# Handing over batch 0's 1 / standard deviation two steps of batch 1's front end earlier, and giving the feed forward's evictions the highest priority

## The chip, the cores and the metric

One Trainium2 chip, one core. The metric is the device time of one execution of the kernel in microseconds. The kernel before takes 1086.92 us, the median of 3 runs from 1086.22 to 1087.01.

## The reference

Eight batches of an attention whose keys and values are averaged over 8 positions, then a block that mixes with a Fourier transform and ends with a feed forward. Cut to what matters, with B = 8, S = 576 positions and 512 channels:

```python
x = attention(q, pooled k, pooled v)          # 8 x 576 x 512
X = np.fft.fft(np.fft.fft(x, axis=1), axis=2)
u = x + np.real(X)
mu = np.mean(u, axis=-1, keepdims=True)
var = np.mean((u - mu) ** 2, axis=-1, keepdims=True)
un = (u - mu) / np.sqrt(var + 1e-06)
ch = np.maximum(un @ w_ch1, 0.0) @ w_ch2      # 512 -> 2048 -> 512
out = u + ch
```

Because the Relu lets a positive factor through, the kernel feeds the centred `u - mu` to the feed forward and multiplies what comes out by `rb`, the 1 / standard deviation. So `rb` is not needed by the first matmul of a block of the feed forward, only after its last one.

## The kernel before, in words

**Two kinds of work.** Each batch b has a front end, the generator `fe(b)`, which yields after each step. Its steps are the scores (psS, L351), their maximum, subtraction and exponential (L356, L365, L367, L368 to L371), transposes (psT, psV, psR), the values (psX, L439, read out by lines 443 to 452), the transform along the channels (psA L558, psB L584, their parts read out at L538) and along the sequence (psQ, psP, L601), the mean (psM, L656 and L657), the centred U (L661) and its two parts `unh` (ScalarE, L645) and `unl` (the rest, L646, two tiles on VectorE and two on GpSimd). Then comes "z", and behind it a tail that makes `rb`. For batch 0 the tail squares (L695 to L698), sums over the partitions with ten small matmuls into psVar (L721), takes the inverse root by three Newton rounds on 128x5 elements (VectorE, L726, L728, L730 to L733), spreads it over a diagonal in X (L736, L737), multiplies that by a matrix of ones (TensorE, L739) and copies it to `rb` (ScalarE, L740).

The feed forward, `ffn`, goes over blocks of columns. One step f of a block takes 128 of the 2048 inner channels. It makes g by twelve matmuls (w1h by unh, w1h by unl, w1low by unh, L775), `hh` = Relu(g) on ScalarE (L779), `hl` = max(g, 0) - hh on VectorE (L780), and then twelve matmuls into four banks acc0 to acc3 (w2h by hh, w2low by hh, w2h by hl, L759). `hh` and `hl` have two buffers each, g has two banks, acc has four banks and no spare: the next block's first matmul into a bank waits for VectorE to have multiplied it by `rb` (L804) and added it to U (L805). Batch 0 has four blocks of eight steps, 288 columns each: (columns 0 to 287, f 0 to 7), (288 to 575, f 0 to 7), then the same two with f 8 to 15. Batches 1 to 6 run in blocks of 384 columns and 16 steps, batch 7 again in blocks of 288. In all 208 steps. In the names, `g_0_7` is step 7 of the block at column 0, `acc_288` or `g_288` the block at column 288.

**Weights.** While batch 0 runs, the weights are prepared chunk by chunk: `prep_w` scales, masks and casts (ScalarE L196, L198, L206; VectorE L201, L202), subtracts on GpSimd (L207) and stores the low part by a DMA of SP's queue (L208). `load_low` reads the low parts back by SP's queue (L217), two steps ahead, for every step.

**What sets the order.** All instructions of an engine run in one order fixed at build time. A scheduler takes, of those instructions whose inputs are there by its own estimate, the one that was traced first, so the tracing order is the priority; a few edges (`issue_after`) pin some of them. The driver traces batch 0's front end as far as "z", then eleven `prep_w`, then batch 1's front end step by step. Among batch 1's steps it hands in the tail of batch 0's: one step (the squares) ahead of step TAIL0, the rest ahead of step TAIL1. From step 20 on, steps of batch 2's front end are handed in too. Only behind all this the feed forward is traced, and so it fills what the front end leaves free. From there on the function `advance` traces later front ends in step with the blocks.

The lines of the driver that count:

```python
fe2, n2 = fe(2), 0
for n, _ in enumerate(fe1):
    if n in (TAIL0, TAIL1):
        next(fe0)
    if n == TAIL1:
        for _ in fe0:
            pass
```

Of the kernel before, what the change touches and what calls it, by code (L numbers as in the profile page):

```python
# [13 lines left out]
AF = mybir.ActivationFunctionType  # L14
ALU = mybir.AluOpType
# [33 lines left out]

AHEAD, LEAD, PACE = 11, 12, 0.65  # L50

TAIL0, TAIL1, NEXT, STEPS = 10, 11, 20, 10
E0, O0, E1, O1 = 0, 1, 2, 3


# [26 lines left out]
def raw(ap):  # L82
    return ap.bitcast(F32)
# [3 lines left out]
def tile_kernel(ctx: ExitStack, tc: tile.TileContext, qt, kt, vm, vr, w1, w2, cad, cbd, mkd, out):  # L87
    nc = tc.nc
# [66 lines left out]
    def high(i, f):  # L155

        if f < 12:
            return whs[i][:, f]
        k = place_of(i, f)
        if k not in tails:  # L160
            tails[k] = wk.tile([P, 2, DM], F32R, tag=f"tail{k}", name=f"w{i + 1}h{f // 2}")
        return tails[k][:, f % 2]
# [51 lines left out]
    def load_low(i, n):  # L214

        lows[i, n] = t = wk.tile([P, DM], F32R, tag="w", bufs=7, name=f"w{i + 1}low")
        nc.sync.dma_start(raw(t), wls[i][:, steps[n]])  # L217
# [528 lines left out]
    def ffn(ro, nb, to, f0, f1):  # L746
        cl = slice(ro, ro + nb)
        end = to + nb == B * S and f1 == NFC
        acc = [pp.tile([P, 512], F32, tag=f"acc{e}", name=f"acc{to}_{f0}_{e}")[:, 0:nb] for e in range(4)]

        def gemm2(f, hh, hl, wh, wl):
            order = [(x, e) for x in range(3) for e in range(4)]
            if f == f1 - 1:
                order = [(x, e) for e in range(4) for x in range(3)]
            for n, (x, e) in enumerate(order):
                w, h = ((wh, hh), (wl, hh), (wh, hl))[x]

                with tc.issue_after(mm.ins) if end and f == f1 - 1 and n and x == 0 else ExitStack():
                    mm = nc.tensor.matmul(acc[e], lhsT=w[:, e], rhs=h, start=(f == f0 and x == 0), stop=(f == f1 - 1 and x == 2))  # L759

        prev = None
        for f in range(f0, f1):
            step = at[0]
            at[0] += 1
            for m in range(2):
                if step + m < len(steps):
                    for i in range(2):
                        if (i, step + m) not in lows:
                            load_low(i, step + m)
            ah, al, bh, bl = [x.rearrange("p (c m) -> p c m", m=P) for x in (high(0, f), lows[0, step], high(1, f), lows[1, step])]  # L770
            ps = pp.tile([P, 512], F32, tag="g1", bufs=2, name=f"g1_{to}_{f}")[:, 0:nb]
            n = 0
            for w, x in ((ah, unh), (ah, unl), (al, unh)):
                for c, ti in enumerate((E0, O0, E1, O1)):
                    nc.tensor.matmul(ps, lhsT=w[:, c], rhs=x[:, ti, cl], start=(n == 0), stop=(n == 11))  # L775
                    n += 1
            hh = wk.tile([P, 384], F32R, tag="hh", bufs=2, name="hh")[:, 0:nb]
            hl = wk.tile([P, 384], F32R, tag="hl", bufs=2, name="hl")[:, 0:nb]
            nc.scalar.activation(hh, ps, AF.Relu)  # L779
            nc.vector.scalar_tensor_tensor(out=hl, in0=ps, scalar=0.0, in1=raw(hh), op0=ALU.max, op1=ALU.subtract)  # L780
            yield
            if prev:
                gemm2(f - 1, *prev)
                yield
            prev = (hh, hl, bh, bl)
        gemm2(f1 - 1, *prev)
        if end:

            last = None
            for e, q in enumerate((nc.sync, nc.scalar, nc.sync, nc.scalar)):  # L790
                u = U[:, e, cl]
                with tc.issue_after(last.ins) if last else ExitStack():
                    last = nc.vector.tensor_tensor(out=X[:, e, 0:nb], in0=acc[e], in1=rb[:, cl], op=ALU.mult)  # L793
                if e % 2:
                    with tc.issue_after(last.ins):
                        last = nc.vector.tensor_tensor(out=u, in0=u, in1=X[:, e, 0:nb], op=ALU.add)
                else:
                    nc.gpsimd.tensor_tensor(out=u, in0=u, in1=X[:, e, 0:nb], op=ALU.add)  # L798
                q.dma_start(out[:, e, to:to + nb], u)
            yield  # L800
            return
        for e in range(4):
            u = U[:, e, cl]
            nc.vector.tensor_tensor(out=acc[e], in0=acc[e], in1=rb[:, cl], op=ALU.mult)  # L804
            nc.vector.tensor_tensor(out=u, in0=u, in1=acc[e], op=ALU.add)  # L805
            if f1 == NFC and e % 2:
                nc.sync.dma_start(out[:, e - 1:e + 1, to:to + nb], U[:, e - 1:e + 1, cl])
        yield
# [72 lines left out]
    for blk in blocks():  # L881
        for _ in ffn(*blk):
            for _ in range(2):
                if done_w < need(pos):
                    prep_w(done_w)
                    done_w += 1
            advance(pos)
            pos += 1
# [109 lines left out]
```

## Time and profile before

| what | value |
|---|---|
| time, median of 3 runs | 1086.92 us |
| the profiled execution's own time | 1087.56 us |
| its span | 1085.6 us |
| its mean granted TensorE clock | 0.991 |
| TensorE matmul (PE) busy | 97% of the span |
| VectorE (DVE) | 57% |
| ScalarE (ACT) | 38% |
| GpSimd (POOL) | 24% |

Times of the trace are microseconds from the start of the span. PE is TensorE's matmul, PEld its weight load, SP the engine that issues the transfers. A row of a timeline gives start, duration and, in brackets, the idle time before it with what ended it. "x4" is four instructions run together into one row; a float32 matmul that is not rounded to fp32r shows twice in the trace, so ten rows of psS in the trace are five matmuls of the program. PEclk is the clock that TensorE was granted, 1.00 at full speed.

### The profile page before, as it was taken

Reading aid. Unit: us, or ns where it says so; the run is one execution under the profiler, and the core shown is the slowest. Engines: PE = TensorE matmul, PEld = TensorE weight load, DVE = VectorE, ACT = ScalarE, POOL = GpSimd, SP = SyncE. Lnnn points to the kernel's source line nnn. Section 1 sums busy time; section 2 is a strip of 40 time slices with the busy share of each in tenths; the row PEclk is TensorE's granted clock in tenths of the full one; section 3 lists DMA queues with packets and bytes.
Section 4 is the critical chain, followed back from the end, with each engine's and each line's share of the span. In section 5 each row is a group of like instructions: output and inputs, shape, how many; then the busy total and the mean of one; then the engine's idle time right before and its main releaser. Section 6 shows DMA issues by size and latency. Waiting matters only on the chain.

```text
span 1085.6 us, 17737 instructions
## 1 busy us (share of the span) xinstructions
PE 1051.1 (97%) x6626; PEld 1016.3 (94%) x6626; DVE 615.3 (57%) x1233; ACT 414.0 (38%) x1083; POOL 256.0 (24%) x264
## 2 busy tenths in 40 slices
PE   8878898999999999999999999999999999999998
PEld 7667688999999999999999999999999999999997
DVE  6698877855376455656376455756467434522122
ACT  5868754443244331533243431443324422311110
POOL 6626365211240032311141032300231101300000
PEclk9889999999999999999999999999999999999999
DMA  8859876655345444444444444445435333346563
GB/s 310 257 186 319 282 259 211 201 177 159 113 120 165 131 153 138 128 141 157 136 124 148 133 150 137 139 131 160 140 106 156 97 106 120 116 129 191 163 190 100
DMA packets 91909, 175.80 MB, mean 162 GB/s; under 512 B 10160, under 2 KB 17328, under 8 KB 91568
## 3 DMA queue, kind: packets, MB, share of 16 engines
q1 hardware_dynamic: 91248, 171.71, 51.0%
q0 software_dynamic: 288, 2.66, 0.6%
q8 instruction: 52, 0.85, 0.3%
q10 hardware_dynamic: 288, 0.30, 0.1%
q14 instruction: 33, 0.27, 0.1%
HBM read 156.81 MB, written 17.83 MB: 161 GB/s over the span
## 4 chain that ended last, share of the span: by engine, by line
PE 86%; DVE 5%; ACT 3%; DMA 3%; POOL 1%; issue 1%; SPq 0%; DVEq 0%; POOLq 0%; ACTq 0%
PE g L775 35%; PE acc L759 35%; PE psX L439 3%; PE psS L351 3%; PE psA L558 2%; PE psP L601 2%; PE psB L584 1%; PE psQ L601 1%; PE psT L392 1%; DMA w2l<-wd 1%; POOL wd L207 1%; DMA w1low<-w1l 1%; ACT wd L198 1%; DMA k<-in_kt 1%; PE psR L415 1%
## 5 line engine op out<-in xcount | busy, mean ns | idle before, releaser
L779 ACT ACTIVATE hh<-g 128x384 fp32r<-128x384 f32 (+1 forms) x208 | 96.6, 464 | 338.1 <-PE g L775 318.4
L780 DVE SCALAR_TENSOR_TENSOR hl<-g,hh 128x384 fp32r<-128x384 f32 (+1 forms) x208 | 108.8, 523 | 189.1 <-ACT hh L779 184.2
L759 PE MATMUL acc<-hh,w2h 128*128 128x384 f32 (+1 forms) x832 | 187.2, 327 | 0.9 <-ACT hh L779 0.7
L759 PE MATMUL acc<-hh,w2low 128*128 128x384 f32 (+1 forms) x832 | 187.3, 327 | 0.0
L775 PE MATMUL g<-unh,w1low 128*128 128x384 f32 (+1 forms) x832 | 181.1, 331 | 4.6 <-DMA w1low<-w1l 4.6
L759 PE MATMUL acc<-hl,w2h 128*128 128x384 f32 (+1 forms) x832 | 182.2, 327 | 0.9 <-DVE hl L780 0.8
L775 PE MATMUL g<-unl,w1h 128*128 128x384 f32 (+1 forms) x832 | 178.2, 328 | 3.0 <-DVE unl L646 3.0
L775 PE MATMUL g<-unh,w1h 128*128 128x384 f32 (+1 forms) x832 | 172.4, 326 | 3.1 <-DVE hl L780 2.3
L775 PEld LDWEIGHTS g<-unh,w1low 128*128 128x128 f32 x832 | 140.1, 190 | 7.8 <-DMA w1low<-w1l 5.9
L759 PEld LDWEIGHTS acc<-hh,w2h 128*128 128x128 f32 x832 | 142.9, 188 | 2.7 <-ACT hh L779 1.8
L775 PEld LDWEIGHTS g<-unh,w1h 128*128 128x128 f32 x832 | 139.7, 189 | 4.6 <-DVE hl L780 2.8
L775 PEld LDWEIGHTS g<-unl,w1h 128*128 128x128 f32 x832 | 139.9, 189 | 4.3 <-DVE unl L646 3.7
L759 PEld LDWEIGHTS acc<-hh,w2low 128*128 128x128 f32 x832 | 143.1, 188 | 0.4 <-issue 0.4
L759 PEld LDWEIGHTS acc<-hl,w2h 128*128 128x128 f32 x832 | 141.6, 189 | 2.0 <-DVE hl L780 1.8
L371 POOL TENSOR_TENSOR t<-t,sm 128x720 f32<-128x720 f32 x32 | 47.4, 1482 | 267.4 <-DVE sm L370 247.2
L286 POOL TENSOR_TENSOR k<-k 128x288 f32<-128x288 f32 (+1 forms) x56 | 37.5, 670 | 84.7 <-DMA k<-in_kt 66.5
L638 POOL TENSOR_TENSOR U<-X,U 128x576 f32<-128x576 f32 (+1 forms) x14 | 19.2, 1375 | 120.3 <-DVE X L620 119.6
L356 DVE TENSOR_REDUCE mx<-psS 128x6 f32<-128x432 f32 x64 | 33.0, 526 | 22.9 <-PE psS L351 22.5
L351 PE MATMUL psS<-kpb,q 128*128 128x144 f32 x280 | 43.3, 291 | 1.6 <-DVE t L365 1.6
L351 PEld LDWEIGHTS psS<-kpb,q 128*128 128x128 f32 x280 | 40.1, 194 | 2.2 <-DVE t L365 1.8
L368 DVE TENSOR_REDUCE sm<-t 128x10 f32<-128x720 f32 x31 | 27.9, 901 | 13.1 <-ACT t L367 12.7
L798 POOL TENSOR_TENSOR U<-U,X 128x288 f32<-128x288 f32 x2 | 1.6, 798 | 140.9 <-DVE X L793 140.9
(218 smaller groups left out, 1466.4 us busy)
## 6 DMA issues: line engine op xcount, KB each, us to landing
w1low<-w1l SPq DMA_DIRECT2D x208, 256.0 KB, 2.7
w2low<-w2l SPq DMA_DIRECT2D x208, 256.0 KB, 2.9
wst<-in_w SPq DMA_DIRECT2D x30, 512.0 KB, 5.1
k<-in_kt SPq DMA_DIRECT2D x28, 288.0 KB, 3.1
q<-in_qt SPq DMA_DIRECT2D x28, 288.0 KB, 3.4
v<-in_vm SPq DMA_DIRECT2D x28, 256.0 KB, 2.9
out<-U SPq DMA_DIRECT2D x18, 384.0 KB, 3.5
w1l<-wd SPq DMA_DIRECT2D x16, 256.0 KB, 4.6
```

Source lines behind the costliest of these rows:

```text
L286: behind["k" if n == 1 and src.shape[1] == J else "v", b] = nc.gpsimd.tensor_tensor(out=out if n == 1 else src[:, :, 0:n], in0=src[:, :, 0 ...
L351: mm = nc.tensor.matmul(ps[:, c * W2J:(c + 1) * W2J], lhsT=q[:, r0:r0 + P], rhs=kpb[g % 2], start=True, stop=True)
L356: nc.vector.tensor_reduce(out=mx[:, c0:c0 + n], in_=pv, op=ALU.max, axis=AX.X, negate=(b, g) in SM)
L368: nc.vector.tensor_reduce(out=sm, in_=t, op=ALU.add, axis=AX.X)
L371: ins = nc.gpsimd.tensor_tensor(out=t, in0=t, in1=sm.unsqueeze(3).broadcast_to([P, 5, 2, J]), op=ALU.mult)
L439: last = nc.tensor.matmul(ps, lhsT=w, rhs=a, start=(i == 0), stop=(i == len(mm) - 1))
L558: last = nc.tensor.matmul(ps, lhsT=w, rhs=a, start=(n == 0), stop=(n == len(mm) - 1))
L601: last = nc.tensor.matmul(ps, lhsT=w, rhs=a, start=(i == 0), stop=(i == 6))
L759: mm = nc.tensor.matmul(acc[e], lhsT=w[:, e], rhs=h, start=(f == f0 and x == 0), stop=(f == f1 - 1 and x == 2))
L775: nc.tensor.matmul(ps, lhsT=w[:, c], rhs=x[:, ti, cl], start=(n == 0), stop=(n == 11))
L779: nc.scalar.activation(hh, ps, AF.Relu)
L780: nc.vector.scalar_tensor_tensor(out=hl, in0=ps, scalar=0.0, in1=raw(hh), op0=ALU.max, op1=ALU.subtract)
```

## The change

Two edits. The constants TAIL0 and TAIL1 go from 10 and 11 to 8 and 9, so that the tail of batch 0's front end is traced behind 8 and 9 steps of batch 1's instead of 10 and 11. And in `ffn`, all 208 Relu evictions `hh` and the 208 `hl` are traced inside `tc.high_priority()`, ahead of everything else in the order of priority; before, they had the low priority of their place in the tracing order. No instruction is added or taken away; the order in which each engine runs them changes from about 71 us on.

```diff
-TAIL0, TAIL1, NEXT, STEPS = 10, 11, 20, 10
+TAIL0, TAIL1, NEXT, STEPS = 8, 9, 20, 10
...
             hh = wk.tile([P, 384], F32R, tag="hh", bufs=2, name="hh")[:, 0:nb]
             hl = wk.tile([P, 384], F32R, tag="hl", bufs=2, name="hl")[:, 0:nb]
-            nc.scalar.activation(hh, ps, AF.Relu)
-            nc.vector.scalar_tensor_tensor(out=hl, in0=ps, scalar=0.0, in1=raw(hh), op0=ALU.max, op1=ALU.subtract)
+            with tc.high_priority():
+                nc.scalar.activation(hh, ps, AF.Relu)
+                nc.vector.scalar_tensor_tensor(out=hl, in0=ps, scalar=0.0, in1=raw(hh), op0=ALU.max, op1=ALU.subtract)
```

The lines behind the second edit stand one lower in the changed kernel: `hh` is L780 there, `hl` L781, the multiplication by `rb` L805 and the addition to U L806.

Three places of the order show it. First TensorE at the end of the tail, where psVar's second pair of matmuls (L739) stands; `g_288_2` is step 2 of batch 0's second block, psT, psV and psR belong to batch 1's front end. Before:

```order
L775 MATMUL g_288_2_1941<-unh,w1h 128x288 x4
L775 MATMUL g_288_2_1941<-unl,w1h 128x288 x4
L775 MATMUL g_288_3_1982<-unh,w1h 128x288 x4
L775 MATMUL g_288_3_1982<-unl,w1h 128x288 x4
L392 MATMUL psT_1_1019<-ident,t_1_946 128x128 x4
L404 MATMUL psV_1_1025<-ident,t_0_881 128x128
L404 MATMUL psV_1_1025<-ident,t_1_946 128x128
L405 MATMUL psV_1_1025<-ident,rt 32x128
L739 MATMUL psVar_981<-X,avg 128x288
L415 MATMUL psR_1_1031<-ident,rt 32x128 x4
L739 MATMUL psVar_981<-X,avg 128x288
```

After, the same place:

```order
L775 MATMUL g_288_1_1900<-unh,w1h 128x288 x4
L775 MATMUL g_288_1_1900<-unl,w1h 128x288 x4
L775 MATMUL g_288_2_1941<-unh,w1h 128x288 x4
L775 MATMUL g_288_2_1941<-unl,w1h 128x288 x4
L739 MATMUL psVar_947<-X,avg 128x288
L775 MATMUL g_288_1_1900<-unh,w1low 128x288 x4
L392 MATMUL psT_0_1011<-ident,t_0_881 128x128 x4
L739 MATMUL psVar_947<-X,avg 128x288
L759 MATMUL acc_0_0_1861<-hh,w2h 128x288
L759 MATMUL acc_0_0_1861<-hh,w2low 128x288
L759 MATMUL acc_0_0_1861<-hl,w2h 128x288
```

psVar's pair now stands one step of the feed forward and a group of transposes earlier, and the second block's first acc matmul comes right behind it; before, four values matmuls (psX) stood between them. The ten small matmuls L721 moved too: before they come behind the last acc matmul of step 7, now behind the values (psX_2) and ahead of the acc matmuls of step 6.

Second ScalarE around `hh` of step 7 of batch 0's first block (`g_0_7`); L196, L198 and L206 are the weights, L331 and L332 belong to batch 1's values. Before:

```order
L447 COPY U<-psX_2_928 1x288
L379 COPY rt<-t_0_881 128x5x16
L448 COPY U<-U 1x288
L198 ACTIVATE wd<-wst 128x512
L779 ACTIVATE hh<-g_0_7_1792 128x288
L198 ACTIVATE wd<-wst 128x512
```

After:

```order
L332 CAST rw_77<-rw_77 32x1
L332 CAST rw_78<-rw_78 32x63
L206 CAST w2h<-wd 128x512
L332 CAST rw_78<-rw_78 32x1
L780 ACTIVATE hh<-g_0_7_1792 128x288
L780 ACTIVATE hh<-g_288_0_1869 128x288
L206 CAST w1h<-wd 128x512
```

`hh` of step 7 now stands behind the copies into rw and behind weight work that followed it before, and right in front of `hh` of the next block's step 0.

Third VectorE at the end of batch 1's first block (columns 576 to 959), where the centred parts of batch 2 (`unl`) are made for the block that follows; `g_576_14` and `g_576_15` are that block's last steps. Before:

```order
L646 TENSOR_TENSOR unl<-X,unh 128x576 x2
L356 TENSOR_REDUCE mx<-psS_2_0_3273 128x6
L365 TENSOR_TENSOR t_2_3270<-psS_2_0_3273,mx 128x432
L356 TENSOR_REDUCE mx<-psS_2_3_3279 128x4
L696 TENSOR_TENSOR X<-X 128x576
L365 TENSOR_TENSOR t_2_3270<-psS_2_3_3279,mx 128x288
L780 SCALAR_TENSOR_TENSOR hl<-g_576_14_3988,hh 128x384
L368 TENSOR_REDUCE sm<-t_2_3270 128x10
L698 TENSOR_TENSOR X<-X 128x576
L780 SCALAR_TENSOR_TENSOR hl<-g_576_15_4021,hh 128x384
```

After:

```order
L646 TENSOR_TENSOR unl<-X,unh 128x576 x2
L356 TENSOR_REDUCE mx<-psS_2_0_3273 128x6
L805 TENSOR_TENSOR acc_0_0_3009<-acc_0_0_3009,rb 128x384
L805 TENSOR_TENSOR acc_0_1_3010<-acc_0_1_3010,rb 128x384
L805 TENSOR_TENSOR acc_0_2_3011<-acc_0_2_3011,rb 128x384
L805 TENSOR_TENSOR acc_0_3_3012<-acc_0_3_3012,rb 128x384
L365 TENSOR_TENSOR t_2_3270<-psS_2_0_3273,mx 128x432
L356 TENSOR_REDUCE mx<-psS_2_3_3279 128x4
L806 TENSOR_TENSOR U<-U,acc_0_0_3009 128x384
L806 TENSOR_TENSOR U<-U,acc_0_1_3010 128x384
L696 TENSOR_TENSOR X<-X 128x576
L806 TENSOR_TENSOR U<-U,acc_0_2_3011 128x384
```

Before, two steps of the feed forward (14 and 15) stand between `unl` and the end of the block; now the block's end comes right behind `unl`. The front ends of the later batches have all moved two steps of the feed forward back in this way.

## The prediction

> **What bounds the kernel now.** The page has TensorE's matmuls busy nearly the whole span, so I read the windows first, to see where they are not.
>
> ```profile
> 100.00:120.00 20.00, 18.86 (x119) 15.38 (x117) 15.17 (x29) 16.47 (x44) 8.82 (x8) 1.00 0.95 328
> 120.00:140.00 20.00, 15.26 (x78) 11.16 (x79) 17.67 (x48) 11.87 (x30) 6.11 (x5) 0.91 0.59 207
> 200.00:220.00 20.00, 20.00 (x155) 19.80 (x155) 16.01 (x46) 8.54 (x21) 2.81 (x2) 1.00 0.57 169
> ```
>
> After the window come its length and the busy time of PE, PEld, DVE, ACT and POOL, then PEclk. From 200 us on a window has 20.00 of 20 us; what can be won lies before. The waits of TensorE say what it waited for, first from 99.8 to 131 us (the tail's stretch), then from 131 to 205 us; from 205 to 1080 us the same view lists none. The columns are total, times, longest.
>
> ```profile
> PE g L775 <- DVE hl L780: 2.3, 2, 1.9
> PE psVar L739 <- DVE X L736: 1.6, 1, 1.6
> PE psT L392 <- DVE t L365: 0.7, 1, 0.7
> PE psV L404 <- ACT ah L397: 0.7, 1, 0.7
> PE g L775 <- DMA w1low<-w1l: 0.6, 1, 0.6
> ```
>
> ```profile
> PE g L775 <- DMA w1low<-w1l: 1.7, 2, 1.0
> PE psB L584 <- DVE B L538: 1.6, 1, 1.6
> PE acc L759 <- DVE hl L780: 0.8, 2, 0.5
> PE acc L759 <- ACT hh L779: 0.5, 1, 0.5
> PE psQ L601 <- DVE AB L546: 0.2, 1, 0.2
> ```
>
> That is 5.9 and 4.8 us. A third loss is the clock:
>
> ```profile
> 125.00:130.00 5.00, 2.76 (x17) 2.12 (x18) 4.79 (x11) 1.90 (x6) 2.32 (x2) 1.00 0.82 285
> 130.00:135.00 5.00, 5.00 (x18) 3.06 (x16) 3.97 (x11) 2.81 (x6) 1.28 (x1) 0.66 0.16 36
> ```
>
> Behind 5 us in which PE was busy 2.76, it gets 0.66 of its clock for 5 us: (1 - 0.66) x 5 = 1.7 us of full-speed work lost. So the stake is 5.9 + 4.8 + 1.7 = 12.4 us, 1.1% of the time. I count 0.2% (2.2 us) as what a measurement of this kernel can tell from no change. The matmuls are the same before and after, so their own time drops out.
>
> **The change part by part.** *The tail's hand-over.* These rows of TensorE show a pair of values matmuls, the tail's start, a wait with its neighbours, and the tail's end; those of VectorE the chain in between and the users of `rb`.
>
> ```profile
> 109.61 0.65 PE L439 MATMUL psX<-ah,wh 128*128 128x288 f32 x2
> 110.18 0.75 PE L439 MATMUL psX<-R,wlo 32*128 32x288 f32 x2
> 118.31 1.17 PE L721 MATMUL psVar<-avg,X 128*128 128x1 f32 x10
> 124.99 0.79 PE L775 MATMUL g<-unh,w1h 128*128 128x288 f32 x4 [1.91 <-DVE hl L780]
> 125.61 0.69 PE L775 MATMUL g<-unl,w1h 128*128 128x288 f32 x4
> 126.14 0.66 PE L392 MATMUL psT<-ident,t 128*128 128x128 f32 x4
> 129.59 0.75 PE L739 MATMUL psVar<-X,avg 128*128 128x288 f32 x2 [1.56 <-DVE X L736]
> ```
>
> ```profile
> 121.61 0.15 DVE L726 TENSOR_SCALAR vv<-psVar 128x5 f32<-128x5 f32 x1
> 121.68 1.52 DVE L202 SCALAR_TENSOR_TENSOR wd<-wst,wd 128x512 int32<-128x512 int32 x1
> 124.85 1.26 DVE L730 TENSOR_TENSOR y<-yy 128x5 f32<-128x5 f32 x1
> 128.84 0.69 DVE L736 TENSOR_TENSOR X<-yy,ident 128x512 f32<-128x512 f32 x1
> 130.81 1.56 DVE L804 TENSOR_TENSOR acc<-acc,rb 128x288 f32<-128x288 f32 x4
> 132.28 1.54 DVE L805 TENSOR_TENSOR U<-U,acc 128x288 f32<-128x288 f32 x4
> ```
>
> The chain from L726 to L736 takes 7.2 us, for a dozen steps on 128x5 elements, of which one takes 0.15 alone and 1.26 at its worst. TensorE waits 1.56 us at its end. Four matmuls of 288 columns take 126.14 - 125.61 = 0.53 us, one psX takes 0.57 + 0.75 = 1.3.
>
> In the changed order I walk TensorE row by row. At 99.8 us it stands where it stood before: earlier differences swap places with waits. From there to L721 come four psX (5.2), 24 matmuls of 288 columns (3.2) and ten short ones of psS (144 columns, priced at 0.09: 0.9), 9.3 us, and 0.4 of wait for `hh` of step 5: L721 starts at about 109.5 instead of 118.3 us. VectorE then runs the chain between work that it also has before: two each of L201 and L202, four L333, three L283, two L356, one L365, two `hl` and L736; at their undisturbed durations 11 us, with two neighbours as slow as the 1.52 and the 1.26 us above 13. X is ready at 121.7 to 123.5 us, 5 to 7 us earlier. But TensorE comes to L739 earlier too: between them lie 56 matmuls of 288 columns (7.4) and ten of psS (0.9); with 0.8 for L721 and 1.65 of waits, below, it is there at 120.3. So the wait at L739 stays, 1.4 to 3.2 us; I take 1.4, since most neighbours in the chain run undisturbed.
>
> Behind it, a wait that is new. Before, four pairs of psX stand between L739 and the next acc matmul; now acc_288 follows at once and needs acc0 to acc3 freed. From L739's start to the first L804 it took 130.81 - 129.59 = 1.22 us, four L804 take 1.56 and the first L805 0.4: bank 0 is free 3.2 us after L739 starts, while TensorE has only 1.3 to 1.7 us to do (psT, w1low, the second L739). That is a wait of 1.5 us; banks 1 to 3 come free with other VectorE work between them (L368, `hl`), another 1.45.
>
> *The priority.* It ranks `hh` and `hl` first among what is ready by the scheduler's estimate; it cannot pass what it placed earlier. So `hh` of step 7 still lands behind rw and weight work:
>
> ```profile
> 117.56 0.95 ACT L331 ACTIVATE rw<-vt,mk 32x63 fp32r<-32x63 f32 x4
> 118.54 0.34 ACT L332 CAST rw<-rw 32x63 fp32r<-32x63 f32 x2
> 119.60 0.78 ACT L198 ACTIVATE wd<-wst 128x512 uint16<-128x512 uint8 x1
> 120.61 0.62 ACT L206 CAST w1h<-wd 128x512 fp32r<-128x512 f32 x1
> 121.84 0.67 ACT L196 ACTIVATE wst<-wst 128x512 f32<-128x512 f32 x1
> ```
>
> One L206, one L196 (0.7), two L198, L331, some 0.8 of L332 and another L206: 0.6 + 0.7 + 1.6 + 0.9 + 0.8 + 0.6 = 5.2 us in front of it, and TensorE has about 4 us of work in that time. I take 1.35 us of wait, and 0.3 for `hl` of step 7. These lie in a stretch where the wait of 1.91 us and that for psT and psV vanish, because g of steps 2 and 3 is no longer asked for before the tail is through.
>
> Sum from 99.8 to 131: 0.4 + 1.35 + 0.3 + 1.4 + 1.5 + 1.45 = 6.4 (5 to 8.2) against 5.9: 0.5 us lost, with ends at 0.9 won and 2.3 lost.
>
> *The clock.* PE's idle time there is spread over more places. If the half-speed piece falls on a stretch that TensorE partly waits through, it costs less: 0 to 1.7, I take 0.9, so 0.8 won. The Trainium skill, "TensorE: Matmul & The Clock Gate", Part 1 and "HAM oscillation", ties the half rate to idle gaps of more than about 3.4 us; by that rule the sum would hold no clock term at all. The trace does not agree: its longest wait in this stretch is 1.91 us, and the clock fell.
>
> *From 131 to 205 us.* The feed forward is over one step further ahead of batch 1's front end. The three waits for `hh` and `hl` (1.3 us) get matmuls of the other kind in front of them and go. The 1.6 at psB has a w1low group between now (0.5): 1.1 stay. w1low of the second half's step 0 (1.0 of the 1.7) is asked for earlier against its store and load: 0.5 to 1.3 are left of it; the other 0.7 falls among more matmuls. I count 1.0 for both and 0.3 for what this walk misses: 1.1 + 1.0 + 0.3 = 2.4 (1.0 to 4.5) for 4.8, so 2.4 won, or 0.3 to 3.8.
>
> *The later blocks.* These rows are from batch 1's first block, where batch 2's centred parts (`unl`) are made.
>
> ```profile
> 309.12 0.30 PE L657 MATMUL psM<-s,avg 128*128 128x288 f32 x1
> 320.28 0.85 PE L775 MATMUL g<-unh,w1h 128*128 128x384 f32 x4
> ```
>
> ```profile
> 309.79 1.30 DVE L661 TENSOR_TENSOR X<-U,psM 128x1152 f32<-128x1152 f32 x1
> 311.83 1.43 DVE L646 TENSOR_TENSOR unl<-X,unh 128x576 fp32r<-128x576 f32 x2 [0.74 <-ACT unh L645]
> 315.25 1.31 DVE L696 TENSOR_TENSOR X<-X 128x576 f32<-128x576 f32 x1
> 318.62 0.75 DVE L698 TENSOR_TENSOR X<-X 128x576 f32<-128x576 f32 x1
> ```
>
> ```profile
> 313.02 2.92 POOL L646 TENSOR_TENSOR unl<-X,unh 128x576 fp32r<-128x576 f32 x2 [1.57 <-ACT unh L645]
> ```
>
> Before, GpSimd's `unl` ends at 315.94, 4.3 us ahead of the block that uses it (320.28). Both move two steps together now: from L657 (T) TensorE has 20 acc matmuls of 384 columns left in the old block, 0.175 us each (0.53 / 4 x 384 / 288), and ten of psS, 4.5 us; fourteen matmuls into the new block it needs the last `unl`, at T + 6.9. If L661 starts at T + 0.25, `unl` ends at T + 6.4: 315.94 - 309.79 is 6.15. So 0.5 us of slack is left where there were 4. The release is as close: the first acc matmul of the new block comes 24 matmuls into the new block, at T + 8.7, one bank each 0.35, and VectorE (two L646, L356, four L805, L365, L356, two L806, L696, two L806; L646 0.7, the others half a microsecond by the four L804 in 1.56 for 288 columns, L696 0.75 like L698) has bank 2 free at T + 9.2 against T + 9.4 needed. With L696 at 1.31 that is 0.4 late, and bank 3 as well. This recurs for batches 4 and 6. Priced at 0.2 each, 0.6 in all; at best 0, at worst 0.8 each.
>
> Sum: -0.5 + 0.8 + 2.4 - 0.6 = 2.1 us won. Ends: 2.3 - 0 - 0.3 + 2.4 = 4.4 lost, 0.9 + 1.7 + 3.8 = 6.4 won. Against the profiled execution's own 1087.56 us it gives 1085.5; that execution is 0.64 over the median of the runs, so I take it from the median: 1086.92 - 2.1 = 1084.8.
>
> **The rivals.** *No change.* The hand-over only trades waits: 8 instead of 6.4 in the tail's stretch, w1low held back by its store. Gain 0.8 + 2.4 - 2.1 - 0.6 = 0.5, so 1086.4. For it speaks that L739's wait stays and that the acc release is new; against it, that the waits after 131 us belong to another stretch. The evictions' priority alone would do nothing from 205 us on, since no wait is there to take away.
>
> *Slower.* The slack of 0.5 us at the boundaries of batches 2, 4 and 6 is gone. If another instruction of GpSimd or VectorE gets between the `unl`, or L661 waits for `hl` and L368 first, as it did before (309.79 is 0.5 after L657 ended), each boundary costs 2 us: 6 lost, 2.7 won earlier, 1090.2. It decides from 0.9 us a boundary on (2.7 / 3) and can be told as slower from 1.6 each ((2.7 + 2.2) / 3). For it: that late L661, and L696 at 1.31 beside GpSimd's `unl`. Against: the changed order puts nothing between the two `unl` at the boundary of batch 2.
>
> *Faster by more.* No wait at L739 and no half-speed piece: 0.9 + 1.7 + 3.8 = 6.4 won less 0.6, 1081.1.
>
> **How the numbers follow.** The forecast, 0 to 4 us won, 0.50; no change, within 1 us of before, 0.18; slower 0.21; faster by more 0.11. The forecast's 2.1 lies at the limit of what can be told: two thirds of it go to faster (0.33) and a third to same (0.17); no change gives 0.16 to same and 0.02 to slower. Faster 0.33 + 0.11 = 0.44, same 0.33, slower 0.23. The range runs from the case of faster by more to short of the slower one's price, and leaves out half of each: 1081.2 to 1089.6.
>
> **What would show it.** Right: L739 starts 5 to 9 us earlier with a wait of 1 to 2 us, a new wait of acc for L806 of 3 us in two pieces behind it, no `hl` wait of 1.9; from 131 to 205 waits of about 2.4; from 205 on less than 1 us. Wrong: waits of g for unl L646 or of acc for L806 around 320, 550 and 780 us of 2 us each, or TensorE's waits from 99.8 to 131 of more than 8.

## The result, and the profile after

The changed kernel takes 1102.32 us, the median of 4 runs from 1099.61 to 1106.43; before takes 1086.72 in the 4 runs beside it. The ratio is 1.0145, with a 95% interval from 1.0111 to 1.0178: slower by 15.6 us, where 2 us faster was forecast and 1089.6 was the upper end of the range. The profiled execution took 1100.04 us with a span of 1098.1, against 1087.56 and 1085.6 before: 12.5 us to be found.

The windows of the changed kernel, columns as before (length, then busy time of PE, PEld, DVE, ACT, POOL, then PEclk):

```profile
100.00:120.00 20.00, 17.79 (x109) 13.91 (x107) 15.71 (x36) 16.78 (x47) 8.47 (x9) 1.00 0.94 335
120.00:140.00 20.00, 17.13 (x109) 15.69 (x110) 16.49 (x36) 12.54 (x27) 6.72 (x5) 0.91 0.75 244
120.00:125.00 5.00, 3.35 (x13) 3.03 (x14) 5.00 (x11) 2.38 (x4) 1.28 (x1) 0.67 0.90 291
160.00:180.00 20.00, 15.68 (x97) 13.82 (x97) 11.16 (x26) 10.71 (x28) 9.73 (x13) 0.83 0.58 177
200.00:220.00 20.00, 17.67 (x128) 16.63 (x127) 18.00 (x34) 10.80 (x29) 5.93 (x6) 1.00 0.48 156
```

120 to 140 us, the tail's window, is fuller than before (17.13 against 15.26 us of PE). 200 to 220, full before, now lacks 2.3 us. From 160 to 180 the mean clock is 0.83, from 120 to 125 it is 0.67. TensorE's waits from 99.8 to 131, from 131 to 205 and from 205 to 1080 us (total, times, longest):

```profile
PE psS L351 <- DVE t L365: 1.8, 1, 1.8
PE acc L759 <- DVE U L806: 1.2, 2, 1.0
PE psS L351 <- ACT R L421: 1.0, 1, 1.0
PE acc L759 <- ACT hh L780: 0.9, 1, 0.9
```

```profile
PE g L775 <- DMA w1low<-w1l: 7.1, 5, 3.6
PE acc L759 <- DVE U L806: 0.2, 1, 0.2
```

```profile
PE acc L759 <- DVE U L806: 2.5, 4, 1.0
PE psV L404 <- DVE al L399: 0.7, 1, 0.7
PE acc L759 <- DVE hl L781: 0.6, 3, 0.2
PE g L775 <- POOL unl L646: 0.6, 2, 0.3
PE acc L759 <- ACT hh L780: 0.6, 1, 0.6
```

The tail's stretch has 4.9 us of waits, less than the 5.9 before. The next has 7.3 for 4.8, nearly all for the low weights. And from 205 us on, where the view listed nothing before, there are now 5.0 us.

Waits do not add up to the whole loss, since a slow clock follows some of them. So I laid the traces against each other by work: each matmul counts with its usual pitch, and the lag is how much later a trace has done the same amount of matmul work as the one before. It is worked out from the start of every matmul, by the time of the kernel before, and the value at 66 us, behind which the first moved instructions fall, is taken off, since the programs reach that point up to 1.5 us earlier or 0.7 later than the kernel before without any change there. Where the order differs, a single value is uncertain by a us or two; across a stretch where all catch up again it is not.

| lag in us at | 155 | 165 | 190 | 210 | 320 | 330 | 590 | 830 | end |
|---|---|---|---|---|---|---|---|---|---|
| both edits, first profile | -2.4 | 4.0 | 4.0 | 6.4 | 6.4 | 7.7 | 9.7 | 12.1 | 12.0 |
| both edits again (e7) | -2.8 | 4.2 | 6.8 | 9.1 | 9.2 | 10.5 | 12.5 | 14.9 | 14.8 |
| first edit alone (e1) | -3.7 | -2.2 | -0.5 | -1.2 | -1.1 | -1.0 | -0.5 | 8.5 | 8.5 |
| second edit alone (e2) | -3.2 | 2.5 | 0.3 | -0.4 | -0.4 | -0.3 | 0.2 | 7.6 | 7.7 |
| low weights first (e4) | -2.4 | -1.3 | -0.7 | -1.5 | -0.9 | 0.6 | 2.5 | 4.9 | 4.9 |
| priority from step 4 (e5) | -2.3 | -0.1 | 2.2 | 1.4 | 1.4 | 1.6 | 1.3 | 1.3 | 1.3 |
| squares on GpSimd (e8) | -1.3 | 3.2 | 4.8 | 7.5 | 8.2 | 8.4 | 11.9 | 14.3 | 14.2 |
| e8 and low weights first (e9) | -1.0 | 1.0 | 1.2 | 0.4 | 0.9 | 1.1 | 6.1 | 7.6 | 7.4 |

The changed kernel is ahead at 155 us, as forecast. Then it loses in steps: about 6 us between 155 and 165 (153 to 170 us in its own trace), 2.4 between 190 and 210 (194 to 217), and 1.3, 2.0 and 2.4 at some 335, 590 and 835 us of its own trace.

**The low weights.** SP's queue of the changed kernel (start, duration, the transfer) and TensorE's rows, at the first and largest loss:

```profile
157.44 0.42 SPq L208 DMA_DIRECT2D w1l<-wd  x1
161.56 0.33 SPq L178 DMA_DIRECT2D wst<-in_w  x1
162.00 1.21 SPq L260 DMA_DIRECT2D k<-in_kt  x1
163.59 0.33 SPq L208 DMA_DIRECT2D w2l<-wd  x1
164.01 0.38 SPq L217 DMA_DIRECT2D w1low<-w1l  x1
```

```profile
164.55 0.53 PE L775 MATMUL g<-unl,w1h 128*128 128x288 f32 x2
168.72 1.33 PE L775 MATMUL g<-unh,w1low 128*128 128x288 f32 x4 [3.65 <-DMA w1low<-w1l]
```

The same load and the matmuls that use it, before:

```profile
167.74 0.38 SPq L217 DMA_DIRECT2D w1low<-w1l  x1
171.31 0.80 PE L775 MATMUL g<-unh,w1low 128*128 128x288 f32 x4 [1.02 <-DMA w1low<-w1l]
```

The load of step 16's first low weight (the first step of batch 0's third block) leaves at 164.01. In front of it in the queue stand a weight load that waited until 161.56 for its buffer, which VectorE's L202 frees, and a store that waited until 163.59 for GpSimd's L207. It lands at 168.68. TensorE was ready for it at 165.1. Before, it left at 167.74 and landed at 171.26, and TensorE was ready at 170.3: the load is earlier by 3.7 us when it leaves and by 2.6 when it lands, but the feed forward is earlier by 5.2. In this stretch the clock falls too:

```profile
165.00:170.00 5.00, 1.35 (x6) 1.21 (x6) 3.13 (x7) 2.32 (x6) 2.13 (x3) 0.61 0.77 243
170.00:175.00 5.00, 5.00 (x29) 4.24 (x28) 1.85 (x5) 4.68 (x13) 3.07 (x3) 0.71 0.46 136
```

In windows of 1 us the clock is still at 1.00 from 165 to 166, falls 1.0 us into the wait, and is at half until some 172.9. So TensorE, busy again from 168.72 on, works for 4.2 us at half speed, which is 2.1 us lost: that is why a wait of 3.65 us costs about 6.

**The block ends.** VectorE of the changed kernel at the end of batch 1's first block:

```profile
327.14 1.43 DVE L646 TENSOR_TENSOR unl<-X,unh 128x576 fp32r<-128x576 f32 x2 [0.74 <-ACT unh L645]
328.49 0.60 DVE L356 TENSOR_REDUCE mx<-psS 128x6 f32<-128x432 f32 x1
329.00 1.95 DVE L805 TENSOR_TENSOR acc<-acc,rb 128x384 f32<-128x384 f32 x4
330.86 0.60 DVE L365 TENSOR_TENSOR t<-psS,mx 128x432 f32<-128x432 f32 x1
331.37 0.45 DVE L356 TENSOR_REDUCE mx<-psS 128x4 f32<-128x288 f32 x1
331.74 1.01 DVE L806 TENSOR_TENSOR U<-U,acc 128x384 f32<-128x384 f32 x2
332.66 1.43 DVE L696 TENSOR_TENSOR X<-X 128x576 f32<-128x576 f32 x1
334.02 1.01 DVE L806 TENSOR_TENSOR U<-U,acc 128x384 f32<-128x384 f32 x2
```

TensorE and GpSimd there:

```profile
334.61 0.44 PE L759 MATMUL acc<-hh,w2h 128*128 128x384 f32 x1 [0.26 <-DVE U L806]
335.91 0.97 PE L759 MATMUL acc<-hl,w2h 128*128 128x384 f32 x4 [0.21 <-DVE hl L781]
```

```profile
332.05 1.43 POOL L697 TENSOR_TENSOR X<-X 128x576 f32<-128x576 f32 x1 [0.51 <-ACT X L695]
```

L696 is slow (1.43 us, not 0.75; GpSimd's L697 runs beside it for 0.8 of that), and it stands in front of the release of banks 2 and 3, so these come free when TensorE already waits. Ahead of batches 4 and 6 L696 takes only 1.02 and 1.01 us. There the second `unl` of VectorE takes 1.58 us, not 0.75, beside GpSimd's `unl`, and it stands in front of three of the four multiplications that free the banks; here ahead of batch 4:

```profile
580.22 1.58 DVE L646 TENSOR_TENSOR unl<-X,unh 128x576 fp32r<-128x576 f32 x1
584.92 1.02 DVE L696 TENSOR_TENSOR X<-X 128x576 f32<-128x576 f32 x1
```

TensorE waits 0.61 us for L806 there, and 0.32 for the last `unl` of GpSimd. Around 215 us, the end of batch 0's third block, the same happens one batch earlier:

```profile
206.81 4.58 DVE L646 TENSOR_TENSOR unl<-X,unh 128x288 fp32r<-128x288 f32 x6
211.32 0.82 DVE L805 TENSOR_TENSOR acc<-acc,rb 128x288 f32<-128x288 f32 x2
214.10 1.26 DVE L696 TENSOR_TENSOR X<-X 128x576 f32<-128x576 f32 x1
215.28 0.81 DVE L806 TENSOR_TENSOR U<-U,acc 128x288 f32<-128x288 f32 x2
```

Batch 1's centred parts, six instructions of VectorE, run directly in front of the release; between 212 and 216 us TensorE waited 0.74 us for `al` (L399, which follows the first releases on VectorE), 0.57 for `hh` and 1.02 for L806.

### The profile page after: what moved, and what is told of

Read it like the earlier page. It is cut to its first block, busy times and chain, and to the rows that moved or that the text cites. A ratio compares the mean times of both kernels' runs of the same rounds, so it can differ in the third digit from the quotient of the medians.

```text
span 1098.1 us, 17732 instructions
## 1 busy us (share of the span) xinstructions
PE 1053.9 (96%) x6626; PEld 1016.1 (93%) x6626; DVE 609.8 (56%) x1233; ACT 413.7 (38%) x1083; POOL 251.7 (23%) x264
## 4 chain that ended last, share of the span: by engine, by line
PE 79%; DVE 10%; DMA 4%; ACT 3%; issue 2%; POOL 1%; SPq 0%; DVEq 0%; ACTq 0%; POOLq 0%
PE acc L759 33%; PE g L775 32%; PE psX L439 3%; PE psS L351 2%; PE psP L601 2%; PE psA L558 2%; PE psB L584 1%; DMA w1low<-w1l 1%; DMA w1l<-wd 1%; PE psQ L601 1%; DVE unl L646 1%; DVE X L661 1%; PE psT L392 1%; DVE wd L202 1%; DVE acc L805 1%
## 5 line engine op out<-in xcount | busy, mean ns | idle before, releaser
L781 DVE SCALAR_TENSOR_TENSOR hl<-g,hh 128x384 fp32r<-128x384 f32 (+1 forms) x208 | 108.6, 523 | 228.6 <-ACT hh L780 227.4
L780 ACT ACTIVATE hh<-g 128x384 fp32r<-128x384 f32 (+1 forms) x208 | 96.6, 465 | 330.8 <-PE g L775 315.3
L759 PE MATMUL acc<-hh,w2h 128*128 128x384 f32 (+1 forms) x832 | 197.8, 334 | 5.4 <-DVE U L806 3.7
L775 PE MATMUL g<-unh,w1low 128*128 128x384 f32 (+1 forms) x832 | 178.4, 330 | 10.0 <-DMA w1low<-w1l 10.0
L775 PE MATMUL g<-unl,w1h 128*128 128x384 f32 (+1 forms) x832 | 174.7, 328 | 3.4 <-DVE unl L646 2.7
L371 POOL TENSOR_TENSOR t<-t,sm 128x720 f32<-128x720 f32 x32 | 45.0, 1408 | 288.8 <-DVE sm L370 275.5
L367 ACT ACTIVATE t<-t 128x720 f32<-128x720 f32 x31 | 24.9, 804 | 40.3 <-DVE t L365 40.2
```

What stands on the lines that cost most here:

```text
L367: nc.scalar.activation(t, t, AF.Exp, scale=1.0 / 64.0)
L371: ins = nc.gpsimd.tensor_tensor(out=t, in0=t, in1=sm.unsqueeze(3).broadcast_to([P, 5, 2, J]), op=ALU.mult)
```

## The experiments

Each diff below is against the changed kernel where nothing else is said. The orders that the kernels are built in narrow the change down before any run. With the priority on `hh` alone, or on the first 32 steps alone, the order of all engines is the same as with both edits. So the second edit acts through `hh` of the first 32 steps and nothing else. How many steps of the feed forward lie ahead of a batch's centred parts also comes from the order; in the lists below these are batches 1 to 7, and the block that uses the parts of batches 2, 4 and 6 begins at step 48, 96 and 144. Before it is 22, 46, 70, 94, 118, 142, 166; with both edits 24, 48, 72, 96, 120, 144, 168.

**e1: the first edit alone**

Against the kernel before:

```diff
-TAIL0, TAIL1, NEXT, STEPS = 10, 11, 20, 10
+TAIL0, TAIL1, NEXT, STEPS = 8, 9, 20, 10
```

> Only TAIL0 and TAIL1 at 8 and 9; hh and hl keep their place in the tracing order. Theory A (the time is lost where the feed forward comes early: 6.6 us at the low weights of step 16 with the slower clock behind them, 3.2 us at the block end after step 24, 5.5 us at the ends of the blocks ahead of batches 2, 4 and 6): the centred parts stand at 22, 46, 71, 96, 120, 144 and 168 steps here, so only the blocks ahead of batches 4 and 6 are without slack; 2 to 4 us are lost there, nothing after step 24, and 0 to 5 at the low weights: 1088 to 1095 us. Rival B (the early hand-over itself costs, by the waits for 1 / standard deviation): nearly all of the 15 us stays, 1099 to 1104.

1096.21 us, ratio 1.0083 (1.0067 to 1.0098). This is 1.2 us above theory A's range and 2.8 below rival B's; the place of the loss speaks for A. Until 820 us it is level with the kernel before, and then it loses 9 us at one place, the end of the block ahead of batch 6. A had 2 to 4 us for the ends ahead of batches 4 and 6 together; the one ahead of batch 4, without slack as well, costs 0.5. TensorE's row and two windows there:

```profile
823.56 0.76 PE L351 MATMUL psS<-kpb,q 128*128 128x144 f32 x4 [2.36 <-DVE X L661]
```

```profile
820.00:825.00 5.00, 2.64 (x17) 1.99 (x15) 5.00 (x11) 1.46 (x3) 0.00 (x0) 0.97 0.18 52
825.00:830.00 5.00, 3.72 (x10) 2.62 (x11) 4.74 (x9) 3.76 (x9) 4.56 (x3) 0.50 0.66 216
830.00:835.00 5.00, 5.00 (x17) 5.00 (x16) 3.40 (x6) 2.47 (x8) 2.78 (x3) 0.50 0.18 52
```

The centring of the second half (L661) comes behind the four L804 on VectorE (1.95 us), and no matmul of the old block is left: 3.6 us of waits (2.36, and 0.40 and 0.88 for `unl`), and 10 us at half the clock from 825 on, in which TensorE was busy 3.72 + 5.00 us, so 4.4 lost. That is 8.0 of the 9.

**e2: the second edit alone**

```diff
-TAIL0, TAIL1, NEXT, STEPS = 8, 9, 20, 10
+TAIL0, TAIL1, NEXT, STEPS = 10, 11, 20, 10
```

> Only hh and hl at the highest priority; TAIL0 and TAIL1 at 10 and 11. Theory A: the centred parts stand at 22, 46, 71, 96, 120, 144 and 167 steps, so 2 to 4 us are lost ahead of batches 4 and 6 and some at the low weights, as the feed forward comes early here too: 1088 to 1097 us. Rival B: without the early hand-over nothing is lost, 1085 to 1088.

1095.85 us, ratio 1.0080 (1.0065 to 1.0095), within theory A's range. The same picture: level until 820 us, then 7.4 us lost at batch 6, with the same wait of 2.4 us for L661. The lag of 2.5 at 165, behind waits of 1.00 us for L511 and 1.26 for low weights and a window from 160 to 165 us at half the clock, is gone by 190. Neither edit alone is slow in the early part, and either alone takes the slack from batches 4 and 6.

**e3: later front ends let in earlier**

```diff
-    free = {1: 0, 2: 64, 3: 128, 4: 160, 5: 224, 6: 256, 7: 320}
+    free = {1: 0, 2: 60, 3: 124, 4: 156, 5: 220, 6: 252, 7: 316}
```

> Both edits, and the table that says at which place of the feed forward a later front end may go on is lower by 4 places (2 steps); the order is the changed kernel's as far as batch 1's first block, and the centred parts of batches 2 to 7 stand some ten steps ahead of their block. Theory A: the 5.5 us at the ends of the blocks ahead of batches 2, 4 and 6 come back, the rest stays: 5 to 6 us faster than the changed kernel, 1094 to 1098. Rival C (the later blocks lose by something else, such as the priority of hh and hl there): less than 2 us come back.

1128.23 us, ratio 1.0384 (1.0365 to 1.0403): neither. This kernel computes something else: with this table a front end may go on before the blocks ahead of it are done with their columns of U. Up to 215 us it repeats the changed kernel (some 6 us go between 155 and 165, some 3 between 190 and 210). Then the front end of batch 2 finds no matmuls of the feed forward beside it: the window from 260 to 280 us has PE at 13.27 and a clock of 0.54, and 19 us go in that part. It says nothing on the block ends.

**e4: the low weights first**

```diff
-        nc.sync.dma_start(raw(t), wls[i][:, steps[n]])
+        with tc.high_priority() if 14 <= n < 24 else ExitStack():
+            nc.sync.dma_start(raw(t), wls[i][:, steps[n]])
```

> Both edits, and the loads of the low weights of steps 14 to 23 at the highest priority; the order is the changed kernel's as far as about 140 us, and the load of step 16's first low weight stands ahead of a store and a load of k in SP's queue. Theory A: it is issued some 2 us earlier, the wait of 3.65 us falls to about 1.7, the clock stays up, 3 to 5 us faster than the changed kernel, 1096 to 1100. Rival D (the load itself is late, since its transfer takes long or its buffer comes free late): no change, 1100 to 1106.

1092.47 us (5 runs from 1090.77 to 1096.88), ratio 1.0056 (1.0033 to 1.0080): 3.5 us under theory A's range. The load left 4.5 us earlier (2.0 of it by an earlier start of that run), behind the weight load but ahead of the store:

```profile
157.84 0.33 SPq L178 DMA_DIRECT2D wst<-in_w  x1
159.48 0.32 SPq L218 DMA_DIRECT2D w1low<-w1l  x1
160.80 0.42 SPq L208 DMA_DIRECT2D w2l<-wd  x1
```

TensorE's waits from 131 to 205 us:

```profile
PE g L776 <- DMA w1low<-w1l: 2.2, 1, 2.2
PE acc L760 <- DVE hl L782: 1.1, 1, 1.1
PE acc L760 <- ACT hh L781: 0.7, 2, 0.4
```

The low weights cost 2.2 us instead of 7.1, and PEclk is 1.00 from 160 to 180 us. The lag at 190 us is -0.7 instead of 4.0, more than expected, and the step at 215 us is gone as well; in this order part of batch 1's centred parts comes a step of the feed forward earlier, behind 23 steps instead of 24. Rival D falls in part only: the transfer took 5.3 us to land, so a late transfer is part of the cost, but not the queue's order alone. What is left are the block ends, 1.5, 1.9 and 2.4 us.

**e5: priority from step 4 on**

```diff
-            with tc.high_priority():
+            with tc.high_priority() if step >= 4 else ExitStack():
```

> Both edits, but hh and hl of steps 0 to 3 keep their old priority. Its order is that of the kernel with the first edit alone as far as step 17 of the feed forward (about 178 us), and then the centred parts stand at 22, 46, 70, 94, 118, 142 and 166 steps, two ahead of their blocks as before the change, where the first edit alone has 71, 96, 120, 144 and 168. Theory A (two steps of slack decide at the block ends): nothing is lost at 590 and 830 us, where the first edit alone lost 0.7 and 8.7: 1085 to 1088 us. Rival E (those losses come from the early hand-over or from the priority): 1093 to 1097.

1087.33 us in 10 runs against 1087.34 before, ratio 0.9999 (0.9984 to 1.0015). The order is e1's as far as step 17, and e1 takes 1096. From 205 us on TensorE has no wait in this trace, and the lag stays at 1.3. Two steps of slack at the later blocks are worth e1's 9 us. Rival E falls.

**e6: priority from step 4 on, the hand-over as before**

Against e5:

```diff
-TAIL0, TAIL1, NEXT, STEPS = 8, 9, 20, 10
+TAIL0, TAIL1, NEXT, STEPS = 10, 11, 20, 10
```

> The second edit without steps 0 to 3, TAIL0 and TAIL1 at 10 and 11: the order before as far as about 205 us, and the centred parts at 22, 46, 70, 94, 118, 142 and 166 steps. Theory A: 1085 to 1088 us, no difference. Rival F (the priority of hh and hl in the later blocks costs by itself): 1090 or more.

1087.00 us, ratio 1.0007 (0.9989 to 1.0025): no difference, and no wait from 205 us on. The priority costs nothing by itself in the later blocks, so rival F falls.

**e7: both edits again**

> The changed kernel once more on this chip. Theory A: 1099 to 1107 us; the late low weights of step 16 and the block ends show again, and what differs from the first profile lies at the low weights, since their transfers end at other times in each run. Rival G (the spread of 7 us between its runs comes from the start of the program): the same waits from 71 us on, another time before.

1100.71 us, ratio 1.0134 (1.0106 to 1.0162). The step at 215 us and the block ends are there again, at the same sizes (2.3, 1.3, 2.0 and 2.4). The low weights vary: 8.5 us of waits from 131 to 205 instead of 7.1, among them 4.05 at step 16 and 2.79 at step 19, where the first profile had 3.65 and 1.39. The spread of this kernel's runs comes at least in part from there, against rival G; the start gave 1.1 us between the two.

**e8: the first addition of squares on GpSimd**

```diff
-        nc.vector.tensor_tensor(out=sq, in0=sq, in1=X[:, 1], op=ALU.add)
+        (nc.gpsimd if b > 1 else nc.vector).tensor_tensor(out=sq, in0=sq, in1=X[:, 1], op=ALU.add)
```

> Both edits, and the first addition of the squares of batches 2 to 7 (L696) on GpSimd instead of VectorE; the order is the changed kernel's as far as the end of batch 1's first block, where L696 no longer stands between the releases of banks 1 and 2. Theory A: L696 took 1.43 us there, so banks 2 and 3 come free 1.4 us earlier and most of the 1.3, 2.2 and 2.4 us lost at about 335, 590 and 835 us goes: 3 to 5 us faster than the changed kernel, 1095 to 1100 for runs like its first profile. Rival H (the centred parts of GpSimd are what comes late there): less than 1.5 us back, and later ends on GpSimd.

1103.14 us, ratio 1.0140 (1.0112 to 1.0167): no gain. At batch 2 the theory holds: L696 no longer stands between the releases, and the lag moves by 0.2 us across this end instead of 1.3. At batches 4 and 6 the order changed again, and VectorE's `unl` came behind releases instead. That less than 1.5 us came back is rival H's number, but what is late is the `unl` of VectorE, not that of GpSimd. TensorE's waits from 200 us on:

```profile
PE g L775 <- DVE unl L646: 3.9, 3, 1.7
PE acc L759 <- DVE U L806: 1.0, 1, 1.0
```

The 3.9 us for `unl` stand where the waits for L806 stood, and 3.5 and 2.4 us are lost there. Without slack one of the two is late; which one is the order's choice.

**e9: e8 with the low weights first**

```diff
+        with tc.high_priority() if 14 <= n < 24 else ExitStack():
+            nc.sync.dma_start(raw(t), wls[i][:, steps[n]])
...
+        (nc.gpsimd if b > 1 else nc.vector).tensor_tensor(out=sq, in0=sq, in1=X[:, 1], op=ALU.add)
```

> The same with the loads of the low weights of steps 14 to 23 at the highest priority too. Theory A: both losses go together, 1086 to 1090 us, the time of the kernel before or a little over it; if it is under 1085, the early part wins what the prediction had counted. Rival H: 1091 to 1095.

1094.53 us, ratio 1.0062 (1.0044 to 1.0080), above what theory A allowed and within what rival H did; again the late parts are mainly VectorE's (2.2 us of waits, 0.3 for GpSimd's). Batch 2 costs 0.2 us, batch 4 now 5.0 (with a clock of 0.84 and 0.81 around it), batch 6 1.5. The two losses are separate, but moving L696 does not mend the block ends.

## Why the prediction was wrong

- **The early part: the total roughly right, the terms not.** From 71 to 99.8 us the waits are 6.5 us for 5.1, where they were said to swap places. The tail's stretch has 4.9 us of waits where 6.4 were counted (5 to 8.2), but 2.8 of these are waits of psS that the sum did not have (1.8 for L365, 1.0 for L421), so it is in part luck that the total came near. L721 starts at 111.69 (109.5 was worked out) and X is ready at 125.1 (121.7 to 123.5). L739 starts at 126.61 without a wait of its own, not after 1.4, because TensorE had waited 1.8 for scores (psS for L365) before it. The new wait for acc is 1.2 in two pieces, not 2.95; `hh` of step 7 waits 0.94 for 1.35 counted. The wait of 1.91 for `hl` went, as forecast.
- **The clock: the term of 0.8 won failed.** The half-speed piece sits at some 121.7 to 125.1 us now (0.50 in the windows of 1 us from 122 to 125), as long as before. It does not overlap the wait of 1.8 us for scores, as the lower price supposed: that wait ends at 121.61, in the row below, and TensorE is busy through the slow piece. In the window from 120 to 125 us (1 - 0.67) x 5 = 1.65 us are lost, against 1.7 before: no gain where 0.8 was counted.

```profile
121.61 1.20 PE L351 MATMUL psS<-kpb,q 128*128 128x144 f32 x4 [1.82 <-DVE t L365]
```

- **From 131 to 205 us: the step that failed first.** It left 0.5 to 1.3 us for the low weight of step 16 and took the others as covered. Step 16 alone waited 3.65, steps 14, 15, 17 and 19 another 3.4, and the half clock from 166 us on made a loss of about 6 us out of the one. The mechanism was named ("asked for earlier against its store and load"); its size was bounded by the wait before. The rows of SP's queue say more: the load sits behind a buffer that VectorE frees and a store that GpSimd releases, both part of the preparation of the weights. These came 3.7 us earlier, the feed forward 5.2. With that position in time, the bound would have been the feed forward's own lead.
- **The end of batch 0's third block was left out.** The prediction looked at the ends ahead of batches 2, 4 and 6, where `unl` is used next. The release of acc is also late where a batch's centring merely runs in front of it: 2.4 us at step 24.
- **The later blocks: right mechanism, wrong size.** The slack is gone and the release of banks 2 and 3 comes late. It was priced at 0.2 a block, 0.8 at worst; it measured 1.3, 2.0 and 2.4. The walk took L696 at 0.75 as its main case, although the 1.31 beside GpSimd's work was quoted; it takes 1.43 ahead of batch 2. It let L661 start 0.25 us behind L657, where it took 0.68, behind `hl` and L370. And it had both `unl` of VectorE at 0.7, where the second takes 1.58 ahead of batches 4 and 6. The slower rival named this place and its point of decision (0.9 us a boundary), and that is the side it fell on; its 2 us a boundary is near the 1.9 measured on average. These 5.7 us less the 2.4 by which the kernel was ahead at 155 us make 1090.2, that rival's time (to the tenth by chance), and the low weights and step 24 put the rest on top.
- **The priority.** It did not "rank `hh` and `hl` first" to any use of its own. What it changed is `hh` of early steps, and with that the phase between the front ends and the blocks. e5 takes just steps 0 to 3 out and the whole loss goes. But the early hand-over without any priority (e1) loses 9 us, so the priority of the steps behind these moves the order too, here to the good; why the scheduler lands on the one phase or the other no run shows.

Still open is how much of the low weights' wait is the queue and how much the transfer. In e4 the load left 4.5 us earlier and landed 3.9 us earlier, of which 2.0 come from the start of that run. And no kernel here beats the one before: e5 and e6 are level with it.

## What to carry to other kernels

When TensorE is full and the order is fixed, ask of a change what it does to the phase between two streams of work, and look at every place where the later stream needs the earlier one, not just at the place that was edited: here two steps of slack at the block ends were worth 9 us in e1. A stream that comes early stops at the next queue that moved by less; place the loads of that queue in time before counting a gain. And price a wait together with the clock: 3.65 us at step 16 cost about 6 and 3.6 us in e1 about 9, since the clock fell, while the 2.2 us of e4 came without a fall.

## What the runs showed of the hardware

- The granted clock fell to 0.50 for some 10 us in e1 (825 to 835 us) after a wait of 2.36 us and a window in which PE was busy 2.64 of 5 us. The Trainium skill, "TensorE: Matmul & The Clock Gate", "HAM oscillation", warns of idle gaps of PE of more than about 3.4 us. These traces do not agree with that as the limit: e1 has no gap so long, and at step 16 the clock was down 1.0 us into the waits of 3.65 us (changed kernel) and 4.05 us (e7).
- The stretches at half clock lasted some 3.4 us (121.7 to 125.1 in the changed kernel), 6.8 (166.1 to 172.9) and 10.2 (824.7 to 835.0 in e1). In the 3.4 us ahead of a fall PE was busy 1.36 us (before, from 127.0), 1.42 (changed, from 118.3), 1.14 (e1, from 821.3) and 2.38 (changed, from 162.7). With 1.81 (before, from 123.6) and 1.88 (e4, from 160.8) the clock stayed up, so the busy share alone does not say when it falls.
- An addition of two 128x576 tiles on VectorE took 0.74 to 0.76 us alone. Beside GpSimd's L697 L696 took 1.01 to 1.43 in the changed kernel and ended some 0.6 us behind it each time (334.09 against 333.48 ahead of batch 2). Beside GpSimd's `unl` and L371, VectorE's `unl` of the same size took 1.08 to 1.97 in several places of e1 and e8, though not in all (0.75 at 695.66 us of e1).
- The low weights of 256 KB took 2.7 us to land in the median of the whole run, but at step 16 4.7 (changed kernel) and 5.3 (e4), when transfers of the weight preparation were in flight; before the change it was 3.5.
